# Attention, expert attention and gated MLP on one core: low halves of two weight matrices moved from VectorE to GpSimd

## The chip, the cores and the metric

The kernel runs on one core of one Trainium2 chip. The metric is the device time of one execution in microseconds (us); the figure to beat is the median of three runs. The core's engines are TensorE (PE, its weight loads PEld), VectorE (DVE), ScalarE (ACT), GpSimd (POOL) and SyncE (SP); each works through a queue of its own in order, and they meet at semaphores. DMAs are issued from the queues of SP, POOL and, a few, ACT.

## What is computed

Three layers in a row, each on 8 batches of 576 positions and 512 channels:

```python
def reference(**kwargs):
    ...
    attn_out = _attn_ref(**attn_kwargs)          # 8 heads of 64, block-causal softmax
    x = ascontiguousarray(attn_out.transpose(0, 2, 1, 3)).reshape(B, S, H * D)
    x = _moe_ref(x=x, **moe_kwargs)              # 4 single-head experts, causal, top 2 by a gate
    return _moe2_ref(x=x, **moe2_kwargs)

def _moe2_ref(x, w_in, w_spatial, b_spatial, w_out):
    h = maximum(x @ w_in, 0.0)
    u, v = halves of h
    v_n = (v - mean(v)) / sqrt(var(v) + 1e-06)
    v_s = einsum('ts,bsd->btd', w_spatial, v_n) + b_spatial
    return (u * v_s) @ w_out
```

Inputs are float32, but w_in and w_out of the last layer come as doubles.

## The kernel before, in words

Every matrix product is made in three f16 products: each operand is split in a high half (its value times a power of two, rounded to f16) and a low half (what the rounding left, also f16), and high x high, high x low and low x high are added in PSUM. The helper split16 (L230) makes such a pair: a scaling into hi on ScalarE, VectorE or GpSimd, then, after a yield, `V.scalar_tensor_tensor(lo, src, scl, hi, ...)` on VectorE (L239).

Per batch there are four attention pairs (two heads each) and two expert pairs. A pair's work goes through scores (PE, row maxima on VectorE, exponentials on ScalarE), weights (L441, the high half of the softmax weights p by a copy on any engine, the low half by a subtraction on VectorE at L451 or on GpSimd at L455, there cut in two), weights_t (L457, a DMA transpose of p into pT, issued by SP), av (PE, L470) and halves (L494, the result pf split into xh and transposed into x by SP). Then come the dense layers: proj, vproj, gate, hv, norm, gating, outp.

Beside batch 0 runs the startup: the weights are loaded, scaled and split. The doubles are turned into f32 in f64 (L525): ScalarE takes the absolute value, VectorE clamps it, shifts, and joins sign and bits in two more operations (L539 to L543), for 12 pieces of 512 columns. The expert output weights are folded into w_in (s_wm), which gives the tile wo in f32, kept in the room of wo16; wout holds the converted w_out. The steps su.wf3 (s_wf3, L754) are the last of the startup: they split these two matrices, each in two pieces of 1024 columns, into wf16 (read by hv at L883 and gating at L964) and wo16 (read by outp at L998). In the profile these tiles read wf<-wo and wo<-wout. A step su.closed after them frees the startup's memory.

The order of the work is written out by hand. add() registers steps, each a generator whose yields cut it into pieces; the tuple ORDER names a step's number each time that its next piece is to be issued, and that sets the order in every engine's queue:

```python
    for i in ORDER:
        t = named[i]
        ...
        run(t)
```

The dictionary WAYS gives, per kind of step and batch, the engine that does it (`"w.0.0"`: the letters of the copy and of the subtraction; `D` VectorE, `A` ScalarE, `G` GpSimd; a last entry stands for the batches behind it). In s_wf3 the engines are fixed, and the change touches this line:

```python
            return split16(w16[:, 0, cs], w16[:, 1, cs], src[:, cs], t["scw", i].bitcast(F32), "A")
```

Of the kernel before, what the change touches and what calls it, by code (L numbers as in the profile page):

```python
# [10 lines left out]
F32 = mybir.dt.float32  # L11
# [25 lines left out]
def attn_moe_gmlp_kernel(  # L37
# [203 lines left out]

    class Obj:
# [115 lines left out]
    def prep_v(b, pr, eng):  # L358
        p, s = PD[b, pr], BS[b]
        t = mine("v")  # L360
        p.v = t.rearrange("p (c h x) -> p h c x", h=2, c=NC)
        o = t.rearrange("p (n x) -> p n x", x=130)
        yield from split16(o[:, :, 0:64], o[:, :, 66:130], p.nat[:, 2].rearrange("p c (h d) -> p (c h) d", h=2),
                           s.sc[:, 2:3], eng)
# [145 lines left out]
    def startup():  # L510
# [14 lines left out]
        def f64(x, src):  # L525
# [19 lines left out]
        def s_win(n):  # L545

            if n < 2:
                t["x", n] = su.tile([P, KD, P], F32, name="x", bufs=2)
            else:
                t["x", n] = t["x", n - 4] if n % 4 < 2 else t["wb"][:, 512 * (n % 2):512 * (n % 2) + 512].rearrange("p (c n) -> p c n", c=KD)  # L550
            return f64(t["x", n], w_in[:, P * n:P * n + P])

        def s_wout(n):
            if n == 0:
                t["wout"] = su.tile([P, KD, DM], F32, tag="woT", name="wout")
            return f64(t["wout"][:, :, P * n:P * n + P], w_out[:, P * n:P * n + P])
# [197 lines left out]
        def s_wf3(i, j):  # L754
# [3 lines left out]
            return split16(w16[:, 0, cs], w16[:, 1, cs], src[:, cs], t["scw", i].bitcast(F32), "A")  # L758
# [6 lines left out]
    def dense(b, keep):  # L765
# [831 lines left out]
```

## Time and profile before

| what | us |
|---|---|
| median of 3 runs | 933.75 (932.49 to 935.44) |
| the profiled execution | 931.44 |
| its span in the profile | 929.7 |
| PE busy in it | 838.6 (90%) |
| VectorE busy | 754.4 (81%) |
| ScalarE busy | 632.9 (68%) |
| GpSimd busy | 547.5 (59%) |

The span is the time from the first to the last instruction of the profiled execution; the profiled execution's own time has some 1.7 us around it. Busy shares are means over stages that differ, so they don't tell what bounds a stage: for that one reads the stages one by one, and which wait ends last there.

### The profile page before, as it was taken

The page shows a single profiled execution, that of the slowest core. Times are in us where ns is not written, and L with a number is a line of the kernel's source. Part 1 is how long each engine was busy: PE and PEld are TensorE (multiplying, and loading weights), DVE is VectorE, ACT ScalarE, POOL GpSimd, SP SyncE. Part 2 cuts the span into 40 slices and gives each one's busy share as a digit, 9 for nine tenths or more (in the row PEclk, how much of TensorE's full clock was granted, in tenths as well). Part 3 has the DMA queues.
Part 4 walks back from the last instruction along what each step waited for, and adds up shares of the span by engine and source line. Part 5 has one row for each costly group of instructions (what it writes and reads, how often), then busy time and mean ns, then how long its engine had stood idle before and what let it go on. Part 6 is the DMA issues. An engine that isn't in the chain of part 4 may idle for free. (4 is left out here: it accounts for less than half of the span.)

```text
span 929.7 us, 25206 instructions
## 1 busy us (share of the span) xinstructions
PE 838.6 (90%) x10038; PEld 616.4 (66%) x10038; DVE 754.4 (81%) x1608; ACT 632.9 (68%) x1151; POOL 547.5 (59%) x542
## 2 busy tenths in 40 slices
PE   3677887789998999989999999989999999999987
PEld 2466765567766767666776677567767786667554
DVE  6999989988998688887988799788997879468351
ACT  3867687866778777785776697675698568448232
POOL 6557457756677767785675867345857665425120
PEclk9777999599999999999999999999999999999999
DMA  9999889998789798999799799879699939914601
GB/s 202 217 220 191 185 178 177 193 158 133 164 152 201 112 186 149 197 189 169 137 159 197 133 149 199 145 138 181 139 180 171 158 58 155 202 30 77 140 1 57
DMA packets 470716, 143.66 MB, mean 155 GB/s; under 512 B 456003, under 2 KB 462499, under 8 KB 470598
## 3 DMA queue, kind: packets, MB, share of 16 engines
q1 hardware_dynamic: 461750, 129.72, 78.4%
q0 software_dynamic: 5232, 11.44, 4.9%
q8 instruction: 79, 1.29, 0.5%
q10 hardware_dynamic: 3616, 0.89, 0.5%
q14 instruction: 39, 0.32, 0.1%
HBM read 38.19 MB, written 9.44 MB: 51 GB/s over the span
## 5 line engine op out<-in xcount | busy, mean ns | idle before, releaser
L455 POOL TENSOR_TENSOR p<-pf,p 128x512 f16<-128x512 f32 (+1 forms) x198 | 242.5, 1247 | 74.7 <-DVE p L354 24.8
L414 DVE TENSOR_REDUCE st<-duo 128x2 f32<-128x1024 f32 (+2 forms) x192 | 151.2, 814 | 17.5 <-PE duo L401 8.8
L470 PEld LDWEIGHTS <-pT 128*128 128x128 f16 x4320 | 144.6, 99 | 28.2 <-DMA pT<-p 12.9
L435 ACT ACTIVATE pf<-duo,st,es 128x512 f32<-128x512 f32 (+3 forms) x224 | 122.4, 617 | 17.0 <-DVE st L426 14.2
L393 PE MATMUL duo<-qk 64*128 64x256 f16 (+3 forms) x1152 | 110.9, 315 | 20.6 <-DVE qk L239 7.7
L356 POOL TENSOR_SCALAR p<-pf 128x1024 f16<-128x1024 f32 (+1 forms) x68 | 78.0, 1149 | 86.5 <-ACT pf L435 55.9
L980 PE MATMUL duo<-wsp,vn 128*128 128x288 f16 x832 | 111.9, 286 | 2.1 <-ACT pf L435 1.1
L470 PE MATMUL duo<-v,pT 128*128 128x65 f16 (+1 forms) x2880 | 102.3, 196 | 10.2 <-DMA pT<-p 5.4
L804 PE MATMUL duo<-x,wqk 128*128 128x288 f16 x768 | 98.7, 286 | 2.1 <-DVE pf L499 0.7
L980 PEld LDWEIGHTS <-vn 128*128 128x128 f16 x832 | 80.0, 98 | 24.0 <-DVE vn L929 1.6
L804 PEld LDWEIGHTS <-wqk 128*128 128x128 f16 x768 | 74.3, 98 | 21.9 <-issue 2.9
L998 PE MATMUL duo<-wo,gT 128*128 128x512 f16 x384 | 86.0, 379 | 0.2 <-POOL gT L987 0.2
L393 PEld LDWEIGHTS <-qk 64*128 64x128 f16 x1152 | 46.2, 98 | 52.5 <-issue 33.0
L921 POOL TENSOR_SCALAR vf<-vf,nw 128x512 f32<-128x512 f32 (+1 forms) x27 | 25.8, 963 | 82.7 <-DVE nw L912 36.6
L435 ACT ACTIVATE pf<-duo,st,mt 128x256 f32<-128x256 f32 (+3 forms) x128 | 69.8, 617 | 5.3 <-DVE st L426 4.0
L451 DVE TENSOR_TENSOR p<-pf,p 128x1024 f16<-128x1024 f32 (+1 forms) x45 | 64.6, 1436 | 6.1 <-ACT p L352 5.8
L998 PEld LDWEIGHTS <-gT 128*128 128x128 f16 x384 | 36.6, 98 | 43.3 <-DVE gT L987 1.0
L504 POOL TENSOR_TENSOR xh<-pf,xh 128x640 f16<-128x640 f32 x30 | 44.8, 1494 | 32.9 <-ACT xh L352 26.6
L827 PE MATMUL duo<-wvg,x 128*128 128x260 f16 x480 | 56.5, 274 | 0.6 <-DVE nw L912 0.6
L352 ACT CAST p<-pf 128x1024 f16<-128x1024 f32 (+1 forms) x53 | 56.7, 1072 | 0.5
L470 PE MATMUL duo<-V,pT 128*128 128x65 f16 (+1 forms) x1440 | 49.6, 194 | 7.8 <-DMA pT<-p 5.2
L883 PE MATMUL duo<-wf,x 128*128 128x512 f16 x240 | 54.5, 379 | 1.8 <-DMA x<-xh 1.2
(273 smaller groups left out, 1732.2 us busy)
## 6 DMA issues: line engine op xcount, KB each, us to landing
out_dram<-pf SPq DMA_DIRECT2D x16, 512.0 KB, 3.3
nat<-in_q_dram SPq DMA_DIRECT2D x40, 128.0 KB, 3.2
nat<-in_k_dram SPq DMA_DIRECT2D x40, 128.0 KB, 3.2
wf<-in_moe_w_in_dram SPq DMA_DIRECT2D x8, 512.0 KB, 5.3
nat<-in_v_dram SPq DMA_DIRECT2D x32, 128.0 KB, 3.0
nat<-in_v_dram POOLq DMA_DIRECT2D x30, 128.0 KB, 4.6
nat<-in_q_dram POOLq DMA_DIRECT2D x22, 128.0 KB, 4.4
nat<-in_k_dram POOLq DMA_DIRECT2D x22, 128.0 KB, 4.4
```

Of the source, the lines that this page charges most:

```text
L352: A.copy(hi, src)
L356: G.tensor_scalar(hi, src, 1.0, 1.0, op0=OP.mult, op1=OP.mult)
L393: T.matmul(ph[:, hh, o:o + w], p.q[hs, a, ts], p.k[hs, bb, 0:w], start=i == 0, stop=False)
L414: V.reduce_max(st[:, 0, 2 * c:2 * c + 2], ph[:, :, off[c]:off[c] + P * (c + 1)], axis=AX.X)
L435: A.activation(pf[:, n * hh + off[c]:n * hh + off[c] + w], ph[:, hh, off[c]:off[c] + w], AF.Exp, bias=st[:, 1, 2 * c + hh:2 * c + hh + 1], ...
L451: V.tensor_sub(lo, src, hi)
L455: G.tensor_sub(lo[:, z:z + m], src[:, z:z + m], hi[:, z:z + m])
L470: T.matmul(ps[:, hh, o:o + n], pT[:, col(t, kk):col(t, kk) + P], p.v[:, hh, kk, a:a + n], start=kk == 0 and i == 0, stop=kk == nk - 1 and ...
L804: T.matmul(ps[:, MID + a:MID + a + w], wqk16[:, l, c, 2 * n + i, :], x16[c][:, r, a:a + w], start=m == 0, stop=m == 11)
L827: T.matmul(ps[:, i, :260], x16[d][:, l, P * c:P * c + P], wvg16[:, r, d, :], start=m == 0, stop=m == 11)
L980: T.matmul(ps[:, MID + a:MID + a + n], l, wsp16[:, r, c, a:a + n], start=i == 0, stop=i == 13)
L998: T.matmul(ps[:, i], gT[:, x, d, P * c:P * c + P], wo16[:, y, d, :], start=m == 0, stop=m == 11)
```

## The change

A new helper split_in has a second way, "P": ScalarE scales the f32 source in place, GpSimd copies it into hi and subtracts hi from it into lo. VectorE has no part in it. Way "D" is the old one. The table uses "P" for the four su.wf3 steps and "D" for the three su.split steps (the first weights); prep_v can take "P" too, but no row of the table does. In f64 the clamp becomes a piece of its own that may stand on GpSimd; the table has VectorE for all twelve. The numbers in ORDER and many letters in WAYS are new.

```diff
+    def split_in(hi, lo, src, scl, way):
+
+        if way == "D":
+            yield from split16(hi, lo, src, scl, "A")
+            return
+        A.mul(src, src, scl)
+        yield
+        G.tensor_scalar(hi, src, 1.0, 1.0, op0=OP.mult, op1=OP.mult)
+        G.tensor_sub(lo, src, hi)
...
-            V.tensor_scalar(x, x, LOW64, HIGH64, op0=OP.max, op1=OP.min)
+            (V if eng == "D" else G).tensor_scalar(x, x, LOW64, HIGH64, op0=OP.max, op1=OP.min)
+            yield
             V.tensor_scalar(xi, xi, 3, 0x3FFFFFFF, op0=OP.logical_shift_left, op1=OP.bitwise_and)
-            yield
...
-        def s_wf3(i, j):
+        def s_wf3(i, j, way):
             w16, src = ((wf16, t["wfu"]), (wo16, t["wout"]))[i]
             n = src.shape[1] // 2
             cs = slice(j * n, j * n + n)
-            return split16(w16[:, 0, cs], w16[:, 1, cs], src[:, cs], t["scw", i].bitcast(F32), "A")
+            return split_in(w16[:, 0, cs], w16[:, 1, cs], src[:, cs], t["scw", i].bitcast(F32), way)
...
+        "su.split.0": ("D",), "su.split.1": ("D",), "su.split.2": ("D",), "su.wf3.0.0": ("P",), "su.wf3.0.1": ("P",),
+        "su.wf3.1.0": ("P",), "su.wf3.1.1": ("P",), "su.win.0": ("D",), "su.win.1": ("D",), "su.win.2": ("D",),
```

The first place in the order is GpSimd's queue in the startup, where the pieces of wf go in. L356 and L455 of before are L366 and L468 of the change, L504 is L517. Before:

```order
L455 TENSOR_TENSOR p_142<-pf,p_142 128x512 x4
L356 TENSOR_SCALAR p_142<-pf 128x1088
L455 TENSOR_TENSOR p_142<-pf,p_142 128x544 x2
L235 TENSOR_SCALAR v<-nat,scb 128x10x64
L356 TENSOR_SCALAR xh<-pf 128x640
```

and with the change:

```order
L468 TENSOR_TENSOR p_142<-pf,p_142 128x512 x4
L366 TENSOR_SCALAR p_142<-pf 128x1088
L468 TENSOR_TENSOR p_142<-pf,p_142 128x544 x2
L249 TENSOR_SCALAR wf_171<-wo_173 128x1024
L250 TENSOR_TENSOR wf_171<-wo_173,wf_171 128x1024
L249 TENSOR_SCALAR wf_171<-wo_173 128x1024
L250 TENSOR_TENSOR wf_171<-wo_173,wf_171 128x1024
L235 TENSOR_SCALAR v<-nat,scb 128x10x64
L366 TENSOR_SCALAR xh<-pf 128x640
```

Four instructions stand new between the low half of the 1088-column tile and the scaling of v. Further on in the same queue, behind a run of loads, before:

```order
L263 DMA nat<-in_k_dram 64x2x64
L455 TENSOR_TENSOR p_142<-pf,p_142 128x512 x2
L356 TENSOR_SCALAR p_142<-pf 128x1024
L455 TENSOR_TENSOR p_142<-pf,p_142 128x512 x2
L455 TENSOR_TENSOR p_142<-pf,p_142 128x544 x2
```

and with the change:

```order
L366 TENSOR_SCALAR xh<-pf 128x640
L284 DMA nat<-in_v_dram 64x2x64 x2
L273 DMA nat<-in_k_dram 64x2x64
L249 TENSOR_SCALAR wo_173<-wout 128x1024
L250 TENSOR_TENSOR wo_173<-wout,wo_173 128x1024
L468 TENSOR_TENSOR p_142<-pf,p_142 128x512 x2
L249 TENSOR_SCALAR wo_173<-wout 128x1024
L250 TENSOR_TENSOR wo_173<-wout,wo_173 128x1024
L366 TENSOR_SCALAR p_142<-pf 128x1024
L468 TENSOR_TENSOR p_142<-pf,p_142 128x512 x2
L468 TENSOR_TENSOR p_142<-pf,p_142 128x544 x2
```

One piece of wo stands ahead of the pair of low halves and one behind it, and a copy of xh, which VectorE had, stands among the loads. The third place is GpSimd's queue at the last batch, the scaling of vf (L921, now L934). Before:

```order
L455 TENSOR_TENSOR p_142<-pf,p_142 128x544 x2
L356 TENSOR_SCALAR xh<-pf 128x640
L504 TENSOR_TENSOR xh<-pf,xh 128x640
L921 TENSOR_SCALAR vf<-vf,nw 128x512 x2
L929 TENSOR_TENSOR vn<-vf,vn 128x512
L987 TENSOR_TENSOR gT<-u,gT 128x576 x2
```

and with the change:

```order
L468 TENSOR_TENSOR p_142<-pf,p_142 128x544 x2
L517 TENSOR_TENSOR xh<-pf,xh 128x640
L934 TENSOR_SCALAR vf<-vf,nw 128x512
L942 TENSOR_TENSOR vn<-vf,vn 128x512
L1000 TENSOR_TENSOR gT<-u,gT 128x576 x2
```

One of the two scalings of vf left GpSimd; it stands on VectorE.

## Rows read from the trace of the kernel before

**Rows 1.** The page's busy tenths in 40 equal slices, PE and VectorE.
```profile
PE   3677887789998999989999999989999999999987
...
DVE  6999989988998688887988799788997879468351
```

**Rows 2.** Busy us by stage: stretch, length, PE, PEld, DVE, ACT, POOL, PE clock, DMA.
```profile
20.00:140.00 120.00, 93.71 (x940) 74.43 (x940) 112.63 (x236) 90.41 (x166) 65.56 (x65) 0.83 0.99 199
140.00:184.00 44.00, 31.10 (x464) 22.92 (x461) 41.92 (x84) 36.12 (x70) 34.69 (x35) 0.76 1.05 188
184.00:200.00 16.00, 13.09 (x244) 11.29 (x242) 13.35 (x25) 9.79 (x19) 5.86 (x6) 0.92 0.99 157
200.00:500.00 300.00, 286.34 (x3615) 211.29 (x3615) 252.00 (x522) 220.59 (x407) 206.98 (x195) 1.00 0.93 164
500.00:800.00 300.00, 289.30 (x3677) 213.73 (x3673) 257.73 (x524) 219.97 (x399) 186.14 (x174) 1.00 0.86 153
```

**Rows 3.** Waits of PE, 140 to 184 us: total us, times, longest us.
```profile
PE duo L393 <- DVE pf L499: 3.6, 1, 3.6
PE duo L393 <- DVE qk L239: 3.1, 2, 2.0
PE duo L470 <- DMA pT<-p: 2.0, 1, 2.0
```

**Rows 4.** Timeline of VectorE, low halves: start us, us, engine, line, what.
```profile
151.15 1.27 DVE L239 SCALAR_TENSOR_TENSOR wf<-wo,scw,wf 128x1024 f16<-128x1024 f32 x1
...
152.40 1.27 DVE L239 SCALAR_TENSOR_TENSOR wf<-wo,scw,wf 128x1024 f16<-128x1024 f32 x1
...
165.74 1.27 DVE L239 SCALAR_TENSOR_TENSOR wo<-wout,scw,wo 128x1024 f16<-128x1024 f32 x1
...
169.82 2.15 DVE L239 SCALAR_TENSOR_TENSOR wo<-wout,scw,wo 128x1024 f16<-128x1024 f32 x1
```

**Rows 5.** VectorE's groups by line and shape: busy us, mean ns, idle before.
```profile
L354 DVE CAST xh<-pf 128x640 f16<-128x640 f32 x13 | 6.8, 521 | 0.2
```

**Rows 6.** ScalarE's groups by line and shape.
```profile
L233 ACT ACTIVATE wf<-wo,scw 128x1024 f16<-128x1024 f32 x2 | 2.3, 1150 | 0.0
```

**Rows 7.** GpSimd's groups by line and shape.
```profile
L455 POOL TENSOR_TENSOR p<-pf,p 128x512 f16<-128x512 f32 x132 | 161.7, 1247 | 51.8 <-DVE p L354 19.7 <-DVE es L324 10.3 <-ACT p L352 7.9
...
L356 POOL TENSOR_SCALAR p<-pf 128x1024 f16<-128x1024 f32 x50 | 56.0, 1121 | 70.1 <-ACT pf L435 46.0 <-issue 12.7 <-DVE p L451 9.1
...
L356 POOL TENSOR_SCALAR xh<-pf 128x640 f16<-128x640 f32 x20 | 15.5, 773 | 29.7 <-DVE pf L499 16.3 <-issue 13.4
```

**Rows 8.** Busy us of each engine from 143.8 to 183.6 us.
```profile
143.80:183.60 39.80, 26.95 (x377) 19.25 (x375) 37.82 (x75) 33.40 (x65) 30.98 (x32) 0.74 1.08 191
```

**Rows 9.** Timeline of GpSimd; in brackets the idle time before, and what ended it.
```profile
166.59 3.29 POOL L455 TENSOR_TENSOR p<-pf,p 128x512 f16<-128x512 f32 x2 [1.83 <-ACT p L352]
169.85 1.03 POOL L356 TENSOR_SCALAR p<-pf 128x1024 f16<-128x1024 f32 x1
...
188.79 1.04 POOL L356 TENSOR_SCALAR p<-pf 128x1024 f16<-128x1024 f32 x1 [5.23 <-ACT pf L435]
...
198.46 1.40 POOL L504 TENSOR_TENSOR xh<-pf,xh 128x640 f16<-128x640 f32 x1 [5.26 <-ACT xh L352]
```

**Rows 10.** Tile wf: ns min/median/max, first and last start us.
```profile
L883 PE MATMUL duo<-wf,x x240: 377/379/390, 219.6 to 884.9; 128*128 128x512 f16 x120
```

**Rows 11.** VectorE's groups by line and shape, as in rows 5.
```profile
L504 DVE TENSOR_TENSOR xh<-pf,xh 128x640 f16<-128x640 f32 x18 | 18.4, 1021 | 0.1
...
L921 DVE TENSOR_SCALAR vf<-vf,nw 128x512 f32<-128x512 f32 x10 | 5.8, 598 | 0.1
...
L237 DVE TENSOR_SCALAR v<-nat,scb 128x640 f16<-128x640 f32 x6 | 4.9, 819 | 0.0
```

**Rows 12.** The chain that ended last, last batch: start us, us, what.
```profile
890.42 2.85 POOL vf L921 x2
...
896.32 2.13 PE duo L980 x16
```

More of the change, by code (lines that the diff above doesn't have):

```diff
@@ L362, in prep_v @@
         o = t.rearrange("p (n x) -> p n x", x=130)
-        yield from split16(o[:, :, 0:64], o[:, :, 66:130], p.nat[:, 2].rearrange("p c (h d) -> p (c h) d", h=2),
-                           s.sc[:, 2:3], eng)
+        x = p.nat[:, 2].rearrange("p c (h d) -> p (c h) d", h=2)
+        if eng == "P":
+            yield from split_in(o[:, :, 0:64], o[:, :, 66:130], x, s.sc[:, 2:3], eng)
+        else:
+            yield from split16(o[:, :, 0:64], o[:, :, 66:130], x, s.sc[:, 2:3], eng)
     LN32 = 3.4657359027997265
@@ L523, in startup, with f64 @@
             tile = staticmethod(lambda *a, **kw: pool["p"].tile(*a, **kw))
-        def f64(x, src):
+        def f64(x, src, eng):
             if src.dtype not in WIDE:
@@ L538, in f64, with s_win @@
             yield
-            V.tensor_scalar(x, x, LOW64, HIGH64, op0=OP.max, op1=OP.min)
+            (V if eng == "D" else G).tensor_scalar(x, x, LOW64, HIGH64, op0=OP.max, op1=OP.min)
+            yield
             V.tensor_scalar(xi, xi, 3, 0x3FFFFFFF, op0=OP.logical_shift_left, op1=OP.bitwise_and)
-            yield
             V.scalar_tensor_tensor(xi, w32[:, :, :, 1], -0x40000000, xi, op0=OP.bitwise_and, op1=OP.bitwise_or)
             V.scalar_tensor_tensor(xi, w32[:, :, :, 0], 29, xi, op0=OP.logical_shift_right, op1=OP.bitwise_or)
-        def s_win(n):
+        def s_win(n, way):
             if n < 2:
@@ L550, in s_win, with s_wout @@
                 t["x", n] = t["x", n - 4] if n % 4 < 2 else t["wb"][:, 512 * (n % 2):512 * (n % 2) + 512].rearrange("p (c n) -> p c n", c=KD)
-            return f64(t["x", n], w_in[:, P * n:P * n + P])
-        def s_wout(n):
+            return f64(t["x", n], w_in[:, P * n:P * n + P], way)
+        def s_wout(n, way):
             if n == 0:
                 t["wout"] = su.tile([P, KD, DM], F32, tag="woT", name="wout")
-            return f64(t["wout"][:, :, P * n:P * n + P], w_out[:, P * n:P * n + P])
+            return f64(t["wout"][:, :, P * n:P * n + P], w_out[:, P * n:P * n + P], way)
         def place(tile_, o, *shape):
@@ L668, in s_cons, with s_split @@
                 G.tensor_copy(y, x)
-        def s_split(i):
+        def s_split(i, way):
             s = sc5.bitcast(F32)[:, i:i + 1]
             if i == 0:
-                return split16(wqk16[:, 0].rearrange("p c e d -> p (c e d)"),
+                return split_in(wqk16[:, 0].rearrange("p c e d -> p (c e d)"),
                                wqk16[:, 1].rearrange("p c e d -> p (c e d)"),
-                               t["wqk"].rearrange("p c g i e d -> p (c g i e d)"), s, "A")
+                               t["wqk"].rearrange("p c g i e d -> p (c g i e d)"), s, way)
             if i == 1:
-                return split16(wvg16[:, 0, :, 0:256], wvg16[:, 1, :, 0:256],
-                               t["wv"].rearrange("p c e d -> p c (e d)"), s, "A")
-            return split16(wvg16[:, 0, :, 256:260], wvg16[:, 1, :, 256:260], t["wg"], s, "A")
+                return split_in(wvg16[:, 0, :, 0:256], wvg16[:, 1, :, 0:256],
+                                t["wv"].rearrange("p c e d -> p c (e d)"), s, way)
+            return split_in(wvg16[:, 0, :, 256:260], wvg16[:, 1, :, 256:260], t["wg"], s, way)
         def s_wsp(c):
@@ L1412, in s1_steps @@
             add(("pv", key), due - 10, lambda w, key=key: prep_v(*key, w),
-                {x: [y, two(640, rate=1.12)] for x, y in (("A", act(640, each=0.2)), ("G", pool(640, rate=1.4)), ("D", cast(640)))},
+                {x: [y, z] for x, y, z in (("A", act(640, each=0.2), two(640, rate=1.12)), ("G", pool(640, rate=1.4), two(640, rate=1.12)),
+                                           ("D", cast(640), two(640, rate=1.12)), ("P", act(640, each=0.2), pool(1920, 2, 1.07)))},
                 [("s2", b)], [], [("v", key)], way="A")
@@ L1503, in attn_moe_gmlp_kernel @@
     if wide:
-        conv += [act(512), ("DVE", 1.05, 0.0, 1), ("DVE", 1.3, 0.0, 1)]
+        conv = {x: conv + [act(512), y, ("DVE", 1.74, 0.0, 1)] for x, y in (("D", ("DVE", 0.39, 0.0, 1)), ("G", ("POOL", 0.56, 0.0, 1)))}
     def sua(n, due, pieces, deps, i=(), acq=(), rel=(), way=None):
@@ L1520, in attn_moe_gmlp_kernel @@
     for i in range(3):
-        sua("split", 17 + i, [act((2048, 1024, 16)[i], each=0.2), two((2048, 1024, 16)[i])], ["scale"], (i,))
+        n = (2048, 1024, 16)[i]
+        sua("split", 17 + i, dict(D=[act(n, each=0.2), two(n)], P=[act(n, each=0.2), pool(3 * n, 2, 1.07)]), ["scale"], (i,), way="D")
     for c in range(NC):
@@ L1528, in attn_moe_gmlp_kernel @@
             sua("win", 34 + 8 * m, conv, ["open"] + (["cons"] + [("wsp", c) for c in range(NC)]) * (m > 1) + [("wm", (m - 4) // 2)] * (m > 3), (m,),
-                ["x64", ("xw", m)], ["x64"])
+                ["x64", ("xw", m)], ["x64"], way="D")
         sua("wm", 48 + 16 * n, [("PE", 3.8), act(512, each=0.05)], [("win", 2 * n), ("win", 2 * n + 1), "woT"], (n,), bk,
@@ L1534, in attn_moe_gmlp_kernel @@
         sua("wout", 100 + 8 * n, conv, [("wm", i) for i in range(4)] + [("wout", 0)] * (n > 0), (n,),
-            ["x64"], ["x64"])
+            ["x64"], ["x64"], way="D")
     for n in range(2):
@@ L1541, in attn_moe_gmlp_kernel @@
         for j in range(2):
-            sua("wf3", 108 + 25 * i + j, [act(1024), two(1024)], [("wf2", i)] + [("wout", n) for n in range(4)], (i, j))
+            sua("wf3", 108 + 25 * i + j, dict(D=[act(1024), two(1024)], P=[act(1024), pool(3072, 2, 1.07)]), [("wf2", i)] + [("wout", n) for n in range(4)], (i, j), way="D")
     sua("closed", 140, [], [("wf3", i, j) for i in range(2) for j in range(2)])
```

408 rows, old and new, of tables (ORDER, WAYS) are left out of this document.

## The prediction

> **What bounds the kernel now.** I read the page's forty slices first, then the busy time by stage, then who waits for whom in the stage that the change touches. In the slices [rows 1] the reader is to see two regimes. From the ninth slice on (a slice is 23.2 us) PE stands at 8 or 9 tenths almost to the end; before that it is mostly at 6 to 8, while VectorE is at 9 from the second slice to the ninth but for one 8. By stage [rows 2]: from 20 to 140 us VectorE is busy 112.63 of 120 us, from 140 to 184 us 41.92 of 44, and PE only 31.10 of those 44. From 200 to 800 us it is the other way round: PE 286.34 and 289.30 of 300 each, VectorE 252.00 and 257.73. So a microsecond of VectorE is worth up to a microsecond before 184 us and close to nothing after 200. The waits agree [rows 3]: what PE waits for between 140 and 184 us is mostly a VectorE result (3.6 us for pf, 3.1 for qk), and once, for 2.0 us, a transposed weight tile pT, whose source is often written by GpSimd.
>
> **The change, part by part.**
>
> *The four low halves.* Before, ScalarE makes each high half and VectorE the low one. VectorE's four instructions stand at 151.15, 152.40, 165.74 and 169.82 us and took 1.27, 1.27, 1.27 and 2.15 us [rows 4], 5.96 us in all, every one inside the stretch in which VectorE is full. They go. In the same stretch one cast of xh goes from VectorE to GpSimd in the new order, 0.52 us [rows 5]. Together 6.5 us leave VectorE before 184 us. Since VectorE's queue stands without a gap there and PE waits for it, I take all of it: **-6.5 us**; the ends are -6.5 and 0 (another engine is as late).
>
> *ScalarE.* Four scalings of 1024 columns into f16 become four of 1024 columns in place, in f32. The nearest row is the f16 form, 1.15 us [rows 6]. Same count, same columns: 0, between -0.5 and +0.5 for all four. They are covered by the 8 us by which ScalarE is short of full in that stage (36.12 of 44 us) [rows 2].
>
> *GpSimd.* Each of the four pieces puts on it a copy of 1024 columns, 1.12 us, and a subtraction of 1024 columns that is not cut in two as those of the softmax weights are: two of 512 columns take 2 x 1.25 = 2.49 us [rows 7]. Four times 3.61 us is 14.5 us; with the xh copy (0.77 us) 15.2 us. In the order two pieces stand behind the low half of a 1088-column tile, at about 143.8 us, where the stretch of [rows 8] begins, and two around the low half that began at 166.59 us [rows 9]. Between 143.8 and 183.6 us GpSimd was busy 30.98 of 39.8 us [rows 8]. With 15.2 more that is 46.2 us, 6.4 more than the stretch has, even if none of its waits remain. The next wait of GpSimd in the trace, 5.23 us ahead of 188.79 us [rows 9], takes up most of that. What is left, 6.4 - 5.2 = **+1.2 us**, I charge to PE, because weight tiles queued behind the pieces reach the transposes that much later and SP's queue takes them in order. Ends: 0 (PE's next use of those tiles has slack) and +6.4 (it has none).
>
> *Who needs the weights.* The first matmul on the folded input weights starts at 219.6 us [rows 10]; the last low half would be written near 177 us. That is no term.
>
> *The two engines in each other's way.* The second wo subtraction on VectorE took 2.15 instead of 1.27 us, 0.88 more [rows 4]; a GpSimd copy of 1.03 us ran beside it, from 169.85 us. The other way round, the pair of GpSimd subtractions at 166.59 us took 3.29 us [rows 9] where a pair takes 2.49 at the mean [rows 7]. So there is a price for standing beside each other, some 0.8 to 0.9 us a time. GpSimd now runs longer instructions through VectorE's busiest stretch. I take two such meetings, **+1.8 us**; ends 0 and four full subtractions, +10 us. The value is nearest to the two stretched rows, since both are meetings of this stage.
>
> [...]
>
> *Elsewhere.* The tables ORDER and WAYS are new throughout. Counted over the program, VectorE also loses four scalings of v at 0.82 us and two subtractions of xh at 1.02 us [rows 11], 5.3 us in all, and two softmax subtractions; GpSimd gains four half subtractions more and issues seven loads fewer, which SP issues. All of that beyond 200 us lies beside a PE that is busy 96% [rows 2]: 0. PE's idle time from 200 to 800 us is 600 - 286.34 - 289.30 = 24.4 us; a new order could win or lose a tenth of it, so the ends are -2.4 and +2.4. The clamp that became its own piece stays on VectorE in all twelve conversions, and so do the low halves of the first weights: the same instructions, 0.
>
> *The last batch.* There the chain runs through two GpSimd scalings of vf, 2.85 us, until PE can go on at 896.32 us [rows 12]. In the new order GpSimd has one of these two and VectorE three instead of two before its first subtraction, at 0.60 us each [rows 11]. GpSimd's chain shortens by half of 2.85, 1.4 us, VectorE's lengthens by 0.6: **-0.7 us**, ends -1.4 and +0.6.
>
> *Sum:* -6.5 + 1.2 + 1.8 - 0.7 = **-4.2 us**. The profiled execution took 931.44 us (span 929.7 and 1.7 around it), so the same execution would take 927.2. The median of the three runs, 933.75, is 2.3 us above it; made against that the forecast is **929.5 us**, 0.45% faster. About 0.3%, 2.8 us, is what a measurement here can tell from no change: faster means below 930.95.
>
> **The rivals.**
>
> *A, GpSimd becomes the bound (slower).* Place: 143.8 to about 200 us. If GpSimd's own waits in that stretch (39.8 - 30.98 = 8.8 us [rows 8]) are for data that comes no earlier, the 15.2 us are not filled into them but come on top. Against them stand the waits of 5.23 and 5.26 us ahead of 188.79 and 198.46 us [rows 9]; 15.2 - 10.5 = 4.7 us stay, and PE, which takes its rows in order, waits that long for pT. The VectorE gain is then worth nothing, since it is not what PE waits for. It decides as soon as the low halves behind the pieces are late by more than the 2.0 us that PE already waits there [rows 3]. For it: 46.2 us of work in a stretch of 39.8. Against it: in [rows 3] two thirds of the waits are for VectorE. Time: 933.75 + 4.7, 938.5 us.
>
> [...]
>
> *C, the gain does not reach the end.* Between 184 and 200 us VectorE is busy 13.35 and PE 13.09 of 16 us [rows 2]: nothing is full, the chain of dependent steps is. An earlier start may be lost there in transposes and loads. Only the last batch's 0.7 us remains: 933 us.
>
> [...]
>
> That the change does not do what it says can be left out: the order shows the eight GpSimd instructions and no low half of wf or wo on VectorE.
>
> **How the numbers follow.** Forecast 0.40, A 0.18, B 0.16, C 0.14, D 0.12. Faster by over 0.3%: D and nearly all of the forecast, 0.49. Within 0.3%: most of B and C and the edge of the forecast, 0.27. Slower: A, and what of B and C falls above 936.55, 0.24. The range has to hold 8 in 10: D's end at 924 (the forecast with the order's -2.4 and the tail's -1.4 comes to about 926), and A's price at the top, 938.5. The forecast's own range is 926 to 932.
>
> **What would show it.** Right: VectorE over 11 us less busy over the program, GpSimd 15 to 20 more; between 140 and 184 us VectorE busy under 38 us, and batch 1's first row on PE after that stage 4 to 6 us earlier; PE's waits on pT there not above 4 us. A would show GpSimd without a gap from 144 to 190 us and PE waiting over 6 us for pT. [...] C would show batch 1 earlier at 184 us and not at 220. The forecast is wrong in its ground if VectorE is not busier than GpSimd in that stage and PE still waits for it.

## The result and the profile after

The changed kernel took 947.04 us (median of 4 runs, 945.80 to 950.94) against 934.60 us for the kernel before beside it: a ratio of 1.0142, interval 1.0106 to 1.0178; the medians are 12.4 us apart. The forecast was 929.5 us in a range up to 938.5, so the time lies outside it and on the other side. The profiled execution took 950.94 us (span 949.2).

The page of the changed kernel, busy tenths in 40 slices (here 23.7 us each), answers to [rows 1]:

```profile
PE   3777896589998999988999989999999999899987
DVE  6899989788797778877788799877998778567361
POOL 6557459955667658685675749326658776314210
```

GpSimd now has two slices of 9 where the change put its work, and PE has its lowest digit of the middle there, a 5. PE's row has an 8 in slices 13, 18, 19 and 24 too; before, slices 13, 15 and 24 have one, so what is new far behind the change are slices 18 and 19, at 403 to 451 us. By stage, as in [rows 2] (stretch, length, busy us and instructions of PE, PEld, DVE, ACT, POOL, then PE's granted clock, DMA share, GB/s):

```profile
20.00:140.00 120.00, 94.08 (x934) 74.72 (x934) 110.44 (x231) 89.09 (x165) 66.12 (x64) 0.87 1.02 198
140.00:184.00 44.00, 27.28 (x442) 21.09 (x441) 37.87 (x73) 35.15 (x67) 43.05 (x41) 0.84 0.92 164
184.00:200.00 16.00, 13.26 (x235) 10.43 (x235) 13.14 (x29) 8.87 (x16) 9.44 (x8) 0.81 1.06 181
200.00:500.00 300.00, 279.54 (x3426) 205.67 (x3426) 241.00 (x503) 215.24 (x400) 196.25 (x185) 0.98 0.86 157
500.00:800.00 300.00, 288.32 (x3670) 213.29 (x3669) 251.04 (x518) 209.78 (x381) 192.60 (x178) 0.99 0.82 152
```

From 140 to 184 us the load moved as forecast: VectorE 37.87 us instead of 41.92, GpSimd 43.05 instead of 34.69, of 44. PE did not gain by it: 27.28 us busy instead of 31.10; by an estimate, busy time times the granted clocks of 0.84 and 0.76, that is some 22.9 us of full clock instead of 23.6. That fall is no sign of the move: experiment 1, the new order without the move, has 27.53 us at 0.79:

```profile
140.00:184.00 44.00, 27.53 (x441) 21.05 (x439) 42.09 (x78) 36.74 (x69) 33.15 (x35) 0.79 0.98 186
```

And from 200 to 500 us PE is busy 279.54 us instead of 286.34, 6.8 us less, at a granted clock of 0.98 instead of 1.00: a second loss, in a stretch that the prediction had put down at nothing.

PE's waits from 140 to 184 us (total us, times, longest us), as in [rows 3]:

```profile
PE duo L483 <- POOL p L468: 4.0, 1, 4.0
PE duo L211 <- DVE pf L512: 3.7, 1, 3.7
PE duo L406 <- DVE gs L870: 3.5, 1, 3.5
PE duo L406 <- DVE qk L239: 2.1, 2, 1.3
```

Without the move (experiment 1) the first two are already there, and shorter, and the third, for gs, is longer (4.4 us):

```profile
PE duo L483 <- POOL p L468: 2.6, 1, 2.6
...
PE duo L211 <- DVE pf L512: 1.2, 1, 1.2
```

The first is put down to a softmax weight on GpSimd. In GpSimd's timeline that weight stands behind one of the new pieces:

```profile
167.44 1.26 POOL L249 TENSOR_SCALAR wo<-wout 128x1024 f16<-128x1024 f32 x1
168.78 2.12 POOL L250 TENSOR_TENSOR wo<-wout,wo 128x1024 f16<-128x1024 f32 x1
170.87 2.27 POOL L468 TENSOR_TENSOR p<-pf,p 128x512 f16<-128x512 f32 x2
...
186.29 2.26 POOL L468 TENSOR_TENSOR p<-pf,p 128x512 f16<-128x512 f32 x2
195.04 1.04 POOL L366 TENSOR_SCALAR p<-pf 128x1024 f16<-128x1024 f32 x1 [6.48 <-issue]
```

Whether the wo piece ahead of 170.87 us is what makes that wait is not shown by this; experiment 11 tries it. GpSimd runs from 140 to 188.5 us with one gap of 0.34 us, and then has one of 6.48, ahead of 195.04 us.

To see where the time went, one event was followed through all traces: PE's first matmul on the folded input weights (wf) in each of the 8 batches, [rows 10] for batch 0 before. Start in us before; the rest is how much later than that:

| batch | 0 | 1 | 2 | 3 | 4 | 5 | 6 | 7 |
|---|---|---|---|---|---|---|---|---|
| before | 219.6 | 324.5 | 424.4 | 528.1 | 631.5 | 732.5 | 816.0 | 877.9 |
| changed | +4.4 | +7.1 | +8.9 | +14.5 | +18.6 | +18.4 | +19.1 | +19.1 |

So some 4 us are lost up to batch 0, then 3, 2, 6 and 4 on the way to batch 4, and nothing afterwards. (The two profiled executions are 19.5 us apart, the medians 12.4. The profiled execution of the kernel before took 931.44 us, where its medians beside the runs below are 935.78 to 937.37; so a lag of 4 to 6 us at the end of a trace can be none in the ratio. Each run below is judged by its ratio, and its trace by where it falls behind.)

### The profile page after: what moved, and what is told of

Its sections match the earlier page's. It is cut to its first block, busy times and chain, and to the rows that moved or that the text cites. A ratio compares the mean times of both kernels' runs of the same rounds, so it can differ in the third digit from the quotient of the medians.

```text
span 949.2 us, 25215 instructions
## 1 busy us (share of the span) xinstructions
PE 844.9 (89%) x10038; PEld 620.0 (65%) x10038; DVE 745.5 (79%) x1598; ACT 633.3 (67%) x1153; POOL 563.3 (59%) x549
## 3 DMA queue, kind: packets, MB, share of 16 engines
q8 instruction: 79, 1.29, 0.6%
## 4 chain that ended last, share of the span: by engine, by line
PE 43%; DVE 8%; DMA 7%; POOL 4%; ACT 3%; issue 2%; SPq 0%; ACTq 0%; POOLq 0%; DVEq 0%
PE duo L817 7%; PE duo L1011 7%; PE duo L483 6%; PE duo L993 6%; DMA pT<-p 5%; PE duo L896 4%; PE duo L840 4%; PE duo L406 3%; PE duo L977 3%; DVE st L427 2%; ACT pf L448 2%; POOL p L468 1%; PE duo L421 1%; PE duo L355 1%; DVE qk L239 1%
## 5 line engine op out<-in xcount | busy, mean ns | idle before, releaser
L468 POOL TENSOR_TENSOR p<-pf,p 128x512 f16<-128x512 f32 (+1 forms) x202 | 244.4, 1234 | 73.9 <-DVE p L364 31.5
L483 PEld LDWEIGHTS <-pT 128*128 128x128 f16 x4320 | 145.5, 99 | 28.6 <-issue 11.4
L366 POOL TENSOR_SCALAR p<-pf 128x1024 f16<-128x1024 f32 (+1 forms) x68 | 81.8, 1204 | 87.4 <-ACT pf L448 52.3
L406 PE MATMUL duo<-qk 64*128 64x128 f16 (+3 forms) x1152 | 111.5, 317 | 24.5 <-DVE qk L239 11.4
L483 PE MATMUL duo<-v,pT 128*128 128x65 f16 (+1 forms) x2880 | 102.6, 196 | 10.7 <-POOL p L468 4.0
L934 POOL TENSOR_SCALAR vf<-vf,nw 128x512 f32<-128x512 f32 (+1 forms) x26 | 22.1, 858 | 90.7 <-DVE nw L925 74.0
L517 POOL TENSOR_TENSOR xh<-pf,xh 128x640 f16<-128x640 f32 x32 | 46.9, 1466 | 32.6 <-ACT xh L362 26.8
L464 DVE TENSOR_TENSOR p<-pf,p 128x1024 f16<-128x1024 f32 (+1 forms) x43 | 55.6, 1293 | 5.8 <-ACT p L362 4.7
L233 ACT ACTIVATE qk<-duo,scb 128x640 f16<-128x640 f32 (+1 forms) x56 | 42.0, 766 | 24.4 <-PE duo L355 22.9
L483 PE MATMUL duo<-V,pT 128*128 128x65 f16 (+1 forms) x1440 | 50.4, 195 | 7.4 <-DMA pT<-p 5.7
```

The lines of the kernel that those rows point to most:

```text
L366: G.tensor_scalar(hi, src, 1.0, 1.0, op0=OP.mult, op1=OP.mult)
L406: T.matmul(ph[:, hh, o:o + w], p.q[hs, a, ts], p.k[hs, bb, 0:w], start=i == 0, stop=False)
L464: V.tensor_sub(lo, src, hi)
L468: G.tensor_sub(lo[:, z:z + m], src[:, z:z + m], hi[:, z:z + m])
L483: T.matmul(ps[:, hh, o:o + n], pT[:, col(t, kk):col(t, kk) + P], p.v[:, hh, kk, a:a + n], start=kk == 0 and i == 0, stop=kk == nk - 1 and ...
```

## The experiments

The two order tables hold the same pieces of work, and at many points the same set of pieces has been issued in both; there one table can be cut and the other joined on. Two theories: **stage** (GpSimd becomes the bound at 143 to 190 us, all else follows from that) and **order** (the new order of the later batches is slower by itself).

**1. The order without the move.** In short:

```diff
-"su.wf3.0.0": ("P",), "su.wf3.0.1": ("P",), "su.wf3.1.0": ("P",), "su.wf3.1.1": ("P",),
+"su.wf3.0.0": ("D",), "su.wf3.0.1": ("D",), "su.wf3.1.0": ("D",), "su.wf3.1.1": ("D",),
```

> The changed kernel with the four last weight pieces back on VectorE: the new order and the new choice of engines, without the move. Theory 'stage' (GpSimd becomes the bound between 143 and 190 us, and what is lost there sets off the rest): near the kernel before, 933 to 937 us, and PE's progress level with before at 300 us and at 600 us. Theory 'order' (the re-planned order of the later batches is itself slower, whatever makes the weights): 942 to 945 us, level with before at 250 us, about 10 us behind at 460 us and 14 us behind at 600 us.

945.76 us against 935.78, ratio 1.0092 (1.0063 to 1.0122). The trace: +0.7 at batch 0, then +3.3, +2.6, +9.4, +12.0, about as "order" had it. The move is gone and two thirds of the loss stay.

**2. The move without the order.** The tables of the kernel before, with the four entries "P".

> The kernel before, in its own order and with its own engines, with nothing changed but the four last weight pieces: scaled in place by ScalarE, both halves by GpSimd. Theory 'stage': all or most of the loss, 942 to 947 us. Theory 'order': only what the stage itself loses, 4 to 5 us, so 938 to 940 us, and that lag stays constant after 200 us. If the prediction was right on the move and only the order spoilt it: 928 to 931 us.

943.63 us, 1.0081 (1.0052 to 1.0110): +8.7 at batch 0, +10.6 from batch 4 on. The number lies in the range of "stage", which experiment 1 contradicts; "order" was too low. In the old order, which was not laid out for it, the move costs about twice what it costs in the new one (experiments 6 to 9). The gain that the prediction saw in the move is not there.

**3. and 4. The tables cut at 200 us.** 821 pieces of one, the rest of the other; each piece has its engine from the table whose order it is in; in the fourth the low halves are VectorE's. In short (the kernels have the joined table written out):

```diff
+    ORDER = ORDER_NEW[:821] + ORDER_OLD[821:]
...
+    ORDER = ORDER_OLD[:821] + ORDER_NEW[821:]
```

> The first 821 pieces of work of the changed kernel (its order, engines and the move, to about 200 us), then the order and engines of the kernel before. Theory 'stage' with a knock-on: 944 to 947 us although the later order is the old one. Theory 'order': 938 to 940 us, 4 to 5 us behind at 200 us and no further behind at 600 us.

> The first 821 pieces of the kernel before (low halves on VectorE), then the order and engines of the changed kernel. Theory 'stage': level with before, 933 to 936 us. Theory 'order': 942 to 944 us, level with before at 250 us and about 14 us behind at 600 us.

New head, old tail: 938.25 us, 1.0012 (0.9989 to 1.0034); +6.2 at batch 0 and +6.0 at batch 4. Old head, new tail: 945.24 us, 1.0089 (1.0058 to 1.0119); +0.7 and +12.5. The later loss belongs to the later order, with or without anything that happens before 200 us.

In both traces with the new tail it arises at the same three places. **First**, near 262 us, in the trace of experiment 1 (start us, us):

```profile
262.28 4.98 DVE L1000 TENSOR_TENSOR gT<-u,gT 128x576 f16<-128x576 f32 x1
...
262.11 0.75 POOL L267 DMA_DIRECT2D nat<-in_q_dram  x1 [0.65 <-PE duo L355]
262.88 2.28 POOL L468 TENSOR_TENSOR p<-pf,p 128x512 f16<-128x512 f32 x2
265.12 1.05 POOL L366 TENSOR_SCALAR p<-pf 128x1024 f16<-128x1024 f32 x1
...
269.03 0.39 PE L406 MATMUL duo<-qk 64*128 64x512 f16 x2 [0.48 <-DVE qk L239]
270.62 0.39 PE L406 MATMUL duo<-qk 64*128 64x512 f16 x2 [1.20 <-DVE qk L239]
```

The gT product took 4.98 us; in the kernel before the same product took 0.75. It stands beside a DMA issue, two subtractions, a copy and a second DMA issue of GpSimd that follow each other without a gap, and the qk halves that PE waits for are queued behind it. **Second**, near 437 us, in the trace of experiment 4 (timeline):

```profile
437.78 1.28 DVE L904 BATCH_NORM_STATS2 bs<-vf 128x6 f32<-128x512 f32 x2
439.79 0.15 DVE L218 TENSOR_SCALAR neh<-duo 128x1 int32<-128x1 int32 x1
...
440.00 4.64 PE L817 MATMUL duo<-x,wqk 128*128 128x288 f16 x24 [3.55 <-DVE neh L218]
```

and the busy time of the same 6 us (columns as by stage above):

```profile
437.00:440.00 3.00, 0.00 (x1) 0.00 (x1) 2.90 (x11) 1.54 (x3) 0.00 (x0) 0.96 0.96 217
440.00:443.00 3.00, 3.00 (x13) 1.87 (x13) 2.22 (x15) 0.00 (x0) 0.40 (x1) 0.50 0.85 176
```

The same rows of the kernel before:

```profile
433.49 0.15 DVE L218 TENSOR_SCALAR neh<-duo 128x1 int32<-128x1 int32 x1
...
433.69 3.10 PE L804 MATMUL duo<-x,wqk 128*128 128x288 f16 x24 [0.34 <-DVE neh L218]
```

A row of 0.15 us, which empties the bank that PE wants next, is queued behind more reductions and the first steps of the normalisation; it starts 6.3 us later than before, in a trace that was 3.1 us behind at batch 2. PE waits 3.55 us, its granted clock stands at 0.50 in the next 3 us (from 431 to 437 us in the kernel before it is 1.00; the changed kernel has 0.50 too, from 446 to 449 us, behind the same wait), and the same 24 matmuls take 4.64 instead of 3.10 us. **Third**, near 541 us, experiment 1:

```profile
541.05 3.09 DVE L857 TENSOR_TENSOR win<-lg 128x5 f32<-128x5 f32 x1
...
540.88 0.80 POOL L267 DMA_DIRECT2D nat<-in_k_dram  x1
541.71 2.39 POOL L468 TENSOR_TENSOR p<-pf,p 128x544 f16<-128x544 f32 x2
...
545.74 2.75 PE L896 MATMUL duo<-wf,x 128*128 128x512 f16 x12 [2.61 <-DVE cmh L203]
```

A product of 5 columns, 0.16 us in the kernel before, starts beside a DMA issue and ends when GpSimd's two subtractions end, and cmh, which PE waits for, is queued behind it.

**5. One entry moved.** In the changed kernel, the step that holds neh goes six entries forward.

```diff
-        770, 771, 771, 522, 526, 526, 526, 756, 525, 526, 770,
+        770, 771, 525, 771, 522, 526, 526, 526, 756, 526, 770,
```

> The changed kernel with one entry of its order table moved: in batch 2 VectorE reads the gating scales out of their bank (neh, L218) ahead of a 1024-column softmax reduction and of the first steps of the normalisation, as the kernel before does, not 6.3 us after PE wrote them. Theory 'this row's place is what PE waits 3.6 us for': the wait of L817 on neh goes, and with it the stretch at the lower clock behind it; 5 us less than the changed kernel, 942 us, and only about 14 us behind at 600 us instead of 18. Rival 'VectorE has no room there, the wait only moves to another row': 946 to 947 us, the lag at 460 us stays at 14 us.

943.58 us, 1.0061 (1.0031 to 1.0091), where the changed kernel had 1.0142 (1.0106 to 1.0178): by the ratios the one entry was worth 0.8%, some 7 us, with wide intervals. PE's wait for that row is what it was before:

```profile
PE duo L817 <- DVE neh L218: 0.3, 1, 0.3
```

The traces say 5.0 us, as expected: between batches 2 and 3 this one loses 0.6 us (7.3 to 7.9), the changed kernel 5.6 (8.9 to 14.5).

**6. to 9. The other two places**, with the move and without it.

```diff
-        "gs.1": ("D", "D", "G", "D", "D", "G", "D", "G"),
+        "gs.1": ("G", "D", "G", "D", "D", "G", "D", "G"),
...
-        452, 213, 556, 324, 210, 556, 459, 460, 552, 458, 461, 437,
+        452, 213, 556, 210, 556, 459, 552, 458, 324, 460, 461, 437,
...
-        687, 815, 684, 803, 917, 905, 893, 899, 815, 684, 893, 686, 687, 933, 687,
+        687, 687, 815, 684, 803, 917, 905, 893, 899, 815, 684, 893, 686, 933, 687,
```

(324 is the gate's step of batch 1, 460 the v half, 815 the gate of batch 4, 687 the column maximum of batch 3.)

> The changed kernel with that entry moved and two more places mended. At 266 us one gT product of batch 1 goes from VectorE, where it took 4.98 us instead of 0.75 beside back-to-back GpSimd instructions, to GpSimd, and one product of the gate and one low half of v go behind the two low halves of qk that PE waits for. At 541 us the column maximum cmh that PE waits for goes ahead of the gate's small products, one of which took 3.09 us instead of 0.16. Theory 'three places make the later loss': 3 us at the first, 5 at the second, 3 at the third; 936 to 937 us, 4 to 6 us behind before from 200 us to the end. Rival 'the later loss is spread over the order': 941 to 943 us, with new lags elsewhere.

> The same as three_places with the four weight pieces on VectorE. Theory 'three places': 933 to 936 us, level with the kernel before from 200 us to the end. Rival 'spread': 939 to 942 us.

940.57 us, 1.0034 (1.0008 to 1.0060), and without the move 937.36 us, 1.0004 (0.9980 to 1.0029), both above what "three places" gave. The first two places are mended (+0.3 at batch 1, +1.6 at batch 2 without the move); the third was not, because the entry moved was that of PE's transposition, not of VectorE's cmh. So again, the other way:

```diff
-        687, 815, 684, 803, 917, 905, 893, 899, 815, 684, 893, 686, 687, 933, 687, 920,
+        687, 684, 803, 917, 905, 893, 899, 684, 893, 686, 687, 933, 687, 815, 815, 920,
```

> As three_places_dve, but the third place mended the other way round: there the row that moved was PE's transposition of hm, and cmh stayed behind the gate's small products on VectorE (one of 1.40 and one of 3.09 us again, the lag went from 1.7 to 4.5 us at 535 us). Here the first gate step goes behind cmh. Theory 'three places make the later loss': no new lag at 535 us, about 2 us behind at the end instead of 5; 934 to 936 us. Rival 'the held product only holds the next row PE needs': 937 us as three_places_dve.

> The same with the move of the low halves (the changed kernel with all three places mended). What is left is the move's own price in the stage at 140 to 200 us: 4 to 6 us behind before from 200 us to the end, 938 to 940 us. Rival 'nothing of it reaches the end': as third_place_dve.

936.61 us, 1.0010 (0.9995 to 1.0026), and 940.18 us, 1.0049 (1.0026 to 1.0071). cmh is now in time, but the trace without the move shows the wait in another place:

```profile
533.84 2.29 DVE L856 TENSOR_TENSOR win<-lg 128x15 f32<-128x15 f32 x1
...
533.68 2.40 POOL L468 TENSOR_TENSOR p<-pf,p 128x544 f16<-128x544 f32 x2
...
540.42 6.04 PE L817 MATMUL duo<-x,wqk 128*128 128x288 f16 x48 [1.90 <-ACT pf L448]
```

Another product of the gate meets the same subtractions, and the softmax reduction behind it is late instead of cmh: batch 4 stays 4.2 us behind. The rival was right there. So two places are mended and the third is not: between batches 3 and 4 the trace without the move still loses 2.9 us (2.6 in experiment 1). The mended places take the order from 1.0092 to 1.0004 and 1.0010 by the ratios, and in the traces from +12.0 at batch 4 to +4.8 and +4.2: most of the later loss is the first two places. The three pairs that differ in the move alone (1.0142 and 1.0092, 1.0034 and 1.0004, 1.0049 and 1.0010) put the price of the move at 0.50, 0.30 and 0.39%, 3 to 5 us; experiment 3, ahead of the old tail, has 0.12% with an interval up to 0.34. (The table behind experiment 14 gives the traces' figure.)

**10. The copies on ScalarE.** On the kernel of experiment 3:

```diff
         A.mul(src, src, scl)
+        A.copy(hi, src)
         yield
-        G.tensor_scalar(hi, src, 1.0, 1.0, op0=OP.mult, op1=OP.mult)
         G.tensor_sub(lo, src, hi)
```

> As head_new_tail_old (938.25 us), but the high half of the four weight pieces is copied by ScalarE and only the subtraction stays on GpSimd: 4.2 us less of copies on GpSimd between 144 and 175 us, some 4.6 us more on ScalarE. Theory 'GpSimd is the bound of the stage' (it stood without a gap from 140 to 188 us): the lag at 200 us falls from 6 us to 2 us, 934 to 936 us. Rival 'the subtractions hold VectorE, the copies cost nothing': no change, 938 us. Rival 'ScalarE is as full' (36 of 44 us): 938 to 941 us, PE waits for rows of ScalarE instead.

937.68 us, 1.0007 (0.9979 to 1.0034): the same as experiment 3; +5.3 at batch 0. From 140 to 184 us GpSimd was down to 39.88 us and ScalarE up from 36.01 to 39.51, and PE's longest wait, ahead of the same rows (L483), was 4.6 us instead of 4.0. The theory that GpSimd's load is the bound is not borne out: 3.2 us less of it bought nothing. That ScalarE's added load ate the gain, as the third rival has it, is not shown: PE's waits that are put down to ScalarE sum to 1.8 us from 140 to 192 us in both traces.

**11. and 12. The pieces in GpSimd's gaps.** On the kernel of experiment 3, GpSimd's two wo pieces moved into the gap ahead of 196 us; then all four into gaps.

```diff
-        165, 164, 393, 47, 161, 166, 165, 298, 396, 399, 288, 392, 291, 169, 299, 291, 166, 400, 48, 290,
+        165, 164, 393, 161, 166, 165, 298, 396, 399, 288, 392, 291, 169, 299, 291, 166, 400, 290,
...
-        310, 310, 292, 160, 421, 186, 311,
+        310, 310, 292, 160, 421, 47, 48, 186, 311,
```

> As head_new_tail_old (938.25 us), but GpSimd's part of the two wo pieces (6.4 us) stands not among the softmax weights at 167 to 176 us but in GpSimd's gap of 6.3 us ahead of 196.63 us. Theory 'lateness' (what the move costs is that softmax weights stand behind the pieces on GpSimd, not the work itself): PE's waits of 4.0 us for pT at 173 us and of 4.05 us for pf at 185 us shrink by 3 us and more each; the lag at 200 us falls from 6 us to 1 to 2 us, 933 to 935 us. Rival 'lock' (a subtraction on GpSimd costs VectorE wherever it stands): 937 to 938 us, the lag arises at 190 to 197 us instead.

> All four pieces of GpSimd in gaps: the two of wf in the gap ahead of 196 us, the two of wo in those at 202 to 212 us. Now nothing stands in front of the softmax weights and VectorE has lost its 6 us before 184 us. Theory 'lateness' with the prediction's VectorE term right: a lag of -4 to -6 us at 190 us, 929 to 932 us. Theory 'lateness' with VectorE's 6 us worth little, because PE waits for chains of steps and not for a full engine: -1 to +1 us, 934 to 936 us. Rival 'lock': 937 us and more.

(47 and 48 are the wo pieces, 186 the first softmax weight behind the gap.) 940.72 us, 1.0022 (0.9999 to 1.0045), and 942.50 us, 1.0043 (1.0023 to 1.0063): not better, +7.8 and +9.1 at batch 0. With the two wo pieces in the gap:

```profile
189.16 1.29 DVE L427 TENSOR_REDUCE st<-duo 128x2 f32<-128x768 f32 x2 [0.23 <-PE duo L414]
190.36 0.64 DVE L226 TENSOR_SCALAR scb<-neb 128x3 int32<-128x3 int32 x1
191.11 0.89 DVE L334 SCALAR_TENSOR_TENSOR es<-inb 128x1 f32<-128x1 f32 x1
192.14 2.64 DVE L364 CAST p<-pf 128x1088 f16<-128x1088 f32 x1
...
188.85 2.13 POOL L250 TENSOR_TENSOR wo<-wout,wo 128x1024 f16<-128x1024 f32 x1
190.95 1.04 POOL L249 TENSOR_SCALAR wo<-wout 128x1024 f16<-128x1024 f32 x1
192.07 2.13 POOL L250 TENSOR_TENSOR wo<-wout,wo 128x1024 f16<-128x1024 f32 x1
...
196.96 1.33 PE L355 MATMUL duo<-ident,nat 128*128 128x128 f32 x5 [3.33 <-DVE qk L239]
```

In the kernel of experiment 3, with the gap empty, the same cast:

```profile
192.60 0.73 DVE L364 CAST p<-pf 128x1088 f16<-128x1088 f32 x1
```

2.64 us instead of 0.73, es 0.89 instead of 0.16, and PE waits 3.33 us for the qk half behind them. The rival "lock" had said just that: the lag arises at 190 to 197 us. The gap was GpSimd's, but it was VectorE's clear run. In experiment 12 the same three rows take the same 0.64, 0.89 and 2.64 us beside the two wf pieces.

"Lateness" had a part too, but not the one that GpSimd's timeline suggested. PE's wait ahead of the 24 matmuls with pT (L483), which is 3.97 us in the changed kernel, is as long in experiment 11 with no wo piece in front of the weights, and shorter in experiment 12, with the wf pieces gone as well (the second line):

```profile
172.64 1.48 PE L483 MATMUL duo<-v,pT 128*128 128x65 f16 x24 [3.98 <-issue]
...
171.48 1.48 PE L483 MATMUL duo<-v,pT 128*128 128x65 f16 x24 [1.90 <-DMA pT<-p]
```

PE's wait for pf fell from 4.0 us in experiment 3 to 2.3 and 2.1.

**13. What VectorE's 6 us are worth.** Order of experiment 11; the low halves of the last two weight matrices are left out.

```diff
-        A.mul(src, src, scl)
+        A.mul(hi, src, scl)
         yield
-        G.tensor_scalar(hi, src, 1.0, 1.0, op0=OP.mult, op1=OP.mult)
-        G.tensor_sub(lo, src, hi)
+        G.memset(lo, 0.0)
```

> What VectorE's 6 us are worth at most: order of wo_in_gap, ScalarE writes the high halves as in the kernel before, and the low halves of the last two weight matrices are left out (GpSimd fills them with zeros, no copy and no subtraction). The prediction's term of -6.5 us: 5 to 6 us ahead of order_only at 190 us, 928 to 931 us. Theory 'chains': at most 1 to 2 us ahead, 933 to 936 us.

935.84 us against 937.37, 0.9988 (0.9965 to 1.0011), and batch 0 at 219.4 us, where the kernel before has 219.6 and experiment 1, with the low halves on VectorE, 220.3 (these 0.9 us are there at 140 us already, as the table behind experiment 14 shows). The stage (columns as by stage above), and PE's longest waits in it:

```profile
140.00:184.00 44.00, 28.72 (x448) 21.62 (x449) 37.86 (x78) 36.20 (x69) 35.24 (x39) 0.81 1.07 187
```

```profile
PE duo L405 <- DVE gs L869: 3.5, 1, 3.5
PE duo L420 <- DVE neb L218: 2.9, 1, 2.9
PE duo L405 <- DVE qk L239: 2.7, 2, 1.8
PE duo L482 <- issue: 1.9, 1, 1.9
```

VectorE is relieved as in the changed kernel (37.86 of 44 us), GpSimd is not loaded (35.24), and next to nothing comes of it. PE still waits 3.5 us for gs, as in the changed kernel. Where the two wf rows stood, VectorE now waits for PE:

```profile
153.99 0.17 DVE L498 TENSOR_SCALAR rr<-duo 128x10 f32<-128x10 f32 x1 [2.60 <-PE duo L482]
```

Up to 182 us it has two more such gaps, 0.92 us for ScalarE and 0.56 for PE; in the kernel before and in experiment 1 it has none in that time. So 4.1 of the 6 us taken off VectorE turned into waiting.

**14. Shorter subtractions.** On the kernel of experiment 3, each `G.tensor_sub` as two of 512 columns.

> As head_new_tail_old (938.25 us), with each of GpSimd's four subtractions cut into two of 512 columns. If a VectorE instruction that meets GpSimd waits for the end of that one instruction, its longest hold halves: 1 to 2 us less, 936 to 937 us, and no VectorE instruction of the stage stretched by more than 1.2 us. If it waits until GpSimd pauses, as the gT product that took 4.98 us beside two subtractions and a copy suggests: no gain, 938 to 939 us, stretches as before.

938.69 us, 1.0031 (1.0011 to 1.0052): no gain. PE's two longest waits are 4.00 and 3.97 us, in experiment 3 3.98 and 4.05. If the tenth percentile of each form over all runs is taken as what a row takes unhindered, VectorE's rows from 140 to 200 us stand 9.6 us above it here and 9.7 in experiment 3; in the kernel before it is 5.3 us, in experiment 1 7.9, in the changed kernel 9.2.

**The stage in all traces.** The runs with the new head share their program up to the first of the four pieces, near 141 us, and yet their traces stand up to 3.8 us apart at 140 us. Only what comes on top behind that belongs to the pieces. Here the same three matmuls of PE are followed: one on wvg, at 139.9 us in experiment 1, one on qk, at 184.3 us, and the first on wf, at 220.3 us. Each entry is how much later than in experiment 1 it starts; the last two columns are less the first.

| run | 139.9 | 184.3 | 220.3 | added by 184 | added by 220 |
|---|---|---|---|---|---|
| changed | +0.8 | +3.3 | +3.8 | 2.6 | 3.0 |
| 3 | +2.2 | +5.1 | +5.6 | 2.9 | 3.4 |
| 5 | 0.0 | +2.5 | +3.6 | 2.5 | 3.6 |
| 6 | +2.8 | +5.4 | +5.9 | 2.5 | 3.1 |
| 9 | +0.6 | +3.2 | +3.9 | 2.6 | 3.3 |
| 10, copies on ScalarE | +1.4 | +4.0 | +4.6 | 2.5 | 3.2 |
| 11, wo in the gap | +1.4 | +3.4 | +7.1 | 2.1 | 5.8 |
| 12, all in gaps | +2.6 | +2.3 | +8.4 | -0.4 | 5.8 |
| 13, left out | -0.9 | -1.3 | -0.9 | -0.4 | 0.0 |
| 14, shorter subtractions | -0.9 | +2.3 | +2.6 | 3.2 | 3.5 |
| 7, low halves on VectorE | 0.0 | 0.0 | 0.0 | 0.0 | 0.0 |
| 8, low halves on VectorE | -0.9 | -0.7 | -0.7 | 0.3 | 0.2 |

Experiments 7 and 8 have the stage of experiment 1 and differ from it by at most 0.3 us behind 140 us. The move costs 3.0 to 3.6 us up to batch 0 wherever the pieces stand at their place in the new order; experiment 2, against the kernel before in the same way, 8.6. Relieving VectorE gives 0.4 us by 184 us, in two different runs (12 and 13), hardly more than that 0.3; in experiment 13, where nothing meets VectorE in the gaps instead, nothing is left of it by 220. For experiment 12 that is what "lateness" with VectorE's 6 us worth little had at 190 us (-1 to +1 us); what comes behind is what "lock" had. Taking the wo pieces out of the stage saves 0.8 us of 2.9, the wf pieces 2.4 more, and standing in the gaps costs more than that.

## Why the prediction was wrong

**The four low halves, -6.5 us: the failed step.** The load left VectorE as computed, but it was worth about nothing: experiment 13 has 0.12% with an interval across zero, and the table above 0.4 us by 184 us and none by 220 (the ends given were -6.5 and 0). The inference from "VectorE's queue stands without a gap there and PE waits for it" to all of it was wrong: PE waits for single rows (gs, neb, qk), and VectorE, once relieved, waits for PE and ScalarE in turn, 4.1 us of the 6. Rival C, which had 0.14, names such chains, but puts them behind 184 us; they hold already inside the stage. The leave-out was run in the new order alone; in the old one, experiment 2 shows only that nothing was left of a gain.

**GpSimd's lateness and the meetings, +1.2 and +1.8 us.** Measured together, 3 to 5 us in the new order by the ratios (1 in experiment 3), 3.0 to 3.6 by the traces, and 7.6 by the ratio in the old order. For the new order the sum of 3.0 is right; that is partly luck, since the place was not: the wait for pT that was to be made by weights behind the wo pieces does not depend on them (experiment 11). The meetings alone are 1.3 us more of held VectorE rows than in experiment 1 (9.2 against 7.9), near the 1.8 taken. The pieces cost a little less than computed (copies 1.04 to 1.26 us, subtractions 2.13 instead of 2.49). GpSimd without a gap from 144 to 188 us is rival A's mark; its other mark, over 6 us of waiting for pT, is not there (4.0, and 2.6 without the move); for a pf it is 3.7 us, and 1.2 without the move. VectorE's subtractions stand at 1.2 to 1.3 us in the stage. Moving the pieces out of the weights' way brought held VectorE rows instead (experiments 11 and 12). How much of PE's loss each of the two makes stays open.

**Elsewhere, 0 with ends of 2.4 us: a second failed step, and the largest error.** The tables were counted by instructions per engine, and these hardly differ; what the new order costs, 0.9%, some 9 us, lies for the most part in where a few rows stand. One of them could have been read from the order alone: neh on VectorE behind two more reductions (5.0 us in experiment 5), with PE's next bank waiting for it. That PE is 96% busy there says that little is waiting now, not that nothing can be: a tenth of its idle time was no bound for a new order.

**ScalarE, 0:** right, 1.16 us in place against 1.15. **The last batch, -0.7** (its two parts add up to -0.8): not there; from batch 7 to the end the changed kernel loses another 0.4 us (19.1 to 19.5). **The clamp, 0:** no loss anywhere near it was seen; it was not tried by itself.

**The rivals.** Chains as in C took the gain, and lateness as in A and held rows are what the stage's loss is left to; how it divides between them is not shown. A's price of 4.7 us with no gain is near what the ratios of experiments 6 and 9 give, 3.2 and 4.6 us. B, with 0.16, is the gain lost to VectorE rows that are held beside GpSimd: there was no gain to lose (experiment 13), and the held rows of the stage are 1.3 us more than in experiment 1, and no less with the subtractions cut in two (9.6 us, and 9.7 without, experiment 14). D, with 0.12, is a higher granted clock, and no run shows its time of 924 us, from which the range was taken: the clock did rise in the stage, from 0.76 to 0.84 (0.79 in experiment 1), and no time came of it (947.04 us, and 945.76 in experiment 1). That a table's re-planned order can lose 9 us by itself was no rival at all.

Of the signs named: GpSimd 15.8 us busier (563.3 against 547.5) and VectorE under 38 us in the stage came as said; VectorE over the whole program is 8.9 us less busy, not over 11; batch 0's wf rows, and with them batch 1, came later, not earlier. (The prediction also reads VectorE's row of tenths as 9 from the second slice to the ninth but for one 8; there are two, in the sixth and the ninth.)

No version tried beats the kernel before.

## What to carry to other kernels

An engine that is full (here VectorE, 41.92 of 44 us) is not yet the bound: before counting its relief as gain, leave the work out in a run and see whether the consumer moves. Two traces of one program can stand some us apart before the changed stage begins (here up to 3.8 us at 140 us), so measure a stage from its own start. A re-planned order is a change of its own; where both orders have issued the same set of work they can be cut and joined, and a few runs tell the order's price from the change's. And in an in-order queue look at the short rows that free a buffer or feed PE: here what stood in front of them set the time, not how long they were (neh takes 0.15 us, and PE waited 3.55 us for it).

## What the runs showed of the hardware

Two VectorE instructions that met GpSimd took longer than any one GpSimd instruction beside them (experiment 1): 4.98 us (0.75 in the kernel before) beside two DMA issues, two subtractions and a copy, of 0.75 to 1.14 us each, and 3.09 us (0.16 in the kernel before) for 5 columns beside a DMA issue of 0.80 us and until the end of two subtractions of 1.20. The cast of experiment 11 took 1.9 us more than in experiment 3, beside a subtraction of 2.13. Halving the length of GpSimd's subtractions did not lessen the held time of the stage (experiment 14: 9.6 against 9.7 us). Reductions of a PSUM bank beside a subtraction (experiment 11, 189.16 us) kept the 1.29 us that they have without one (experiment 3). So in these rows a cast and two-input products were stretched, by 1.9, 4.2 and 2.9 us, and the reductions were not; the cast's stretch is about as long as the one subtraction beside it, those of the two products are longer. What sets the length of a stretch is not shown.
